# Three projections of a GEGLU feed-forward block: 2x2 blocks by seven products of block sums in place of eight block products

## The chip, the cores and the metric

The kernel runs on one core of one Trainium2 chip. The metric is the device time of one execution in microseconds (us); a run's state is told from its time and from the clock granted to TensorE. Below, "head" is what runs before the loop over column blocks or pairs, and "tail" what follows the last matmul. Engines are named PE (TensorE matmul), PEld (TensorE weight load, which overlaps PE), DVE (VectorE), ACT (ScalarE), POOL (GpSimd) and SP (SyncE, which here only issues DMAs). "Bank" is one of the eight PSUM banks of 128 x 512 fp32.

## The reference

```python
B, S, D, F = 32, 32, 1024, 3584            # all inputs bfloat16, normal * 0.05
def reference(x, w_gate, w_up, w_down):
    return (gelu_tanh(x @ w_gate) * (x @ w_up)) @ w_down
```

There are N = B*S = 1024 tokens. In units of 128x128 weights by 512 moving columns, gate and up cost 28 column blocks x 2 matrices x 2 token halves x 8 contraction blocks = 896 matmuls, and down costs 8 token blocks x 2 column halves x 28 contraction blocks = 448.

## The kernel before

The first four column blocks of gate and up run while inputs still arrive. Then comes one column block after the other, with the weights as the stationary operand, and both token halves after one weight load (`held` means that the weights stay in the array; this cut and the next have comments added):

```python
for m in range(4, FM):                      # FM = 28 column blocks of 128
    b0 = 4 * (m % 2)
    for kind, b in (("g", b0), ("u", b0 + 1)):
        for k in range(DK):                 # DK = 8
            for h in range(2):
                mm_gu(kind, m, h, k, b + 2 * h, held=h == 1)
    for h in range(2):
        glu(m, h, b0 + 2 * h, b0 + 2 * h + 1)   # ACT: gelu(bank) to SBUF; DVE: times bank -> hT
    # ... DMA loads of later weights (cut)

jobs = [[(tc, 0, 512), (tc, 512, 512)] for tc in range(TC - 1)]
jobs += [[(TC - 1, 0, 512)], [(TC - 1, 512, 416)], [(TC - 1, 928, 96)]]
for job in jobs:
    for m in range(FM):
        for i, (tc, col, n) in enumerate(job):
            # matmul: hT block (tc, m) stationary, wd[m] moving, held for the second column half
            ...
    # ACT or DVE copies each bank to SBUF as bfloat16, SP sends it out (cut)
```

## Time and profile before

| quantity | value | view |
|---|---|---|
| time | 299.25 us, median of 4 (299.12 to 299.92) | runs beside the changed kernel |
| span of the profiled execution | 297.9 us | page |
| PE busy, DVE busy, ACT busy | 294.5, 42.7, 37.3 us | page, engines |
| matmuls of the program | 1372, worth 1344 of 512 columns | page, groups |
| gate and up after the first 4 blocks | 33.1 to 198.9 us: 165.7 us | starts in the timeline |
| down, PE only | 198.9 to 295.6 us: about 96.7 us | starts in the timeline |

From the page of the kernel before: the engines (busy us, share of the span, instructions), the granted clock in 40 slices, and the chain that ended last ("issue" is time in which the profile shows nothing to wait for; a q after an engine means its sequencer).

```profile
PE 294.5 (99%) x1388; PEld 77.9 (26%) x808; DVE 42.7 (14%) x68; ACT 37.3 (13%) x67; POOL 0.7 (0%) x6
...
PEclk9999999999999999999999999999999999999999
...
PE 96%; DMA 2%; SPq 0%; issue 0%; ACT 0%
```

The list of waits of PE (engine, line, waited for: us in total, times, longest):

```profile
PE ps L98 <- PEq L310: 0.8, 1, 0.8
PE ps L98 <- DMA xT<-in_x_dram: 0.5, 1, 0.5
```

Groups of instructions with the shapes kept apart (count after the x; then busy us and mean ns of one; then idle time before them and what ended it):

```profile
L98 PE MATMUL ps<-xT,wg 128*128 128x512 bf16 x256 | 90.4, 380 | 0.5 <-DMA xT<-in_x_dram 0.5
...
L163 PE MATMUL ps<-xT,wg 128*128 128x512 bf16 x192 | 72.8, 379 | 0.0
...
L98 DVE TENSOR_TENSOR hT<-g,ps 128x512 bf16<-128x512 f32 x56 | 36.3, 685 | 159.0 <-PE ps L98 159.0
...
L98 PEld LDWEIGHTS ps<-xT,wg 128*128 128x128 bf16 x256 | 25.0, 98 | 72.4 <-issue 64.0 <-DMA wg<-in_w_gate_dram 1.0 <-DVE xT L98 0.3
...
L98 DVE CAST xT<-ps 128x512 bf16<-128x512 f32 x7 | 4.8, 692 | 79.8 <-ACT xT L98 79.8
...
L98 DVE CAST xT<-ps 128x416 bf16<-128x416 f32 x1 | 0.6, 592 | 9.8 <-PE ps L98 9.8
```

A matmul's record lasts 380 ns, but records overlap; what it costs is the distance between starts. The timeline of PE (start, length, what, count) shows that:

```profile
12.38 1.03 PE L98 MATMUL ps<-xT,wg 128*128 128x512 bf16 x4
13.24 1.03 PE L98 MATMUL ps<-xT,wu 128*128 128x512 bf16 x4
```

Four matmuls take 13.24 - 12.38 = 0.86 us; by the finer start times it is 0.2158 each, which the prediction takes as 0.2157. 1344 of them are 289.9 us. PE has nothing to wait for, so the span is a count of matmuls times 0.2157, plus about 8 us at the two ends. Held matmuls (line 163) and those with a weight load (line 98) last the same: the load of 98 ns is hidden.

### The profile page before, as it was taken

The numbers are of one execution on the slowest core, as the hardware profiler recorded it, in microseconds if no ns is written. First come the engines' busy times: TensorE is split into PE (matmuls) and PEld (weight loads), VectorE is DVE, ScalarE is ACT, GpSimd is POOL, SyncE is SP. The second block draws the span as 40 slices with busy tenths as digits, with TensorE's granted clock in tenths as the row PEclk, the third lists the DMA queues.
The fourth block names the chain that finished last, engine by engine and source line by source line (L and its number), as shares of the span: only waits on it lengthen the run. The fifth ranks groups of instructions, "written<-read, shape, count | busy, mean of one in ns | idle before, by whom it ended". The sixth has DMA issues, their size and how long they took to land.

```text
span 297.9 us, 2578 instructions
## 1 busy us (share of the span) xinstructions
PE 294.5 (99%) x1388; PEld 77.9 (26%) x808; DVE 42.7 (14%) x68; ACT 37.3 (13%) x67; POOL 0.7 (0%) x6
## 2 busy tenths in 40 slices
PE   8999999999999999999999999999999999999997
PEld 4444322222222222222222222222222222222244
DVE  1030311111222111111111122110000000000000
ACT  1030411111111111121111111110000000000010
POOL 0000000000000000000000000000000000000000
PEclk9999999999999999999999999999999999999999
DMA  7999743005707509312030030000101101011011
GB/s 164 275 216 357 246 153 108 35 0 187 236 2 264 160 1 315 109 50 91 0 132 11 0 141 0 0 2 0 35 0 35 37 0 35 0 37 35 0 35 35
DMA packets 28874, 26.37 MB, mean 89 GB/s; under 512 B 8384, under 2 KB 25280, under 8 KB 28864
## 3 DMA queue, kind: packets, MB, share of 16 engines
q1 hardware_dynamic: 26640, 24.25, 26.2%
q10 hardware_dynamic: 2224, 1.97, 2.7%
q8 instruction: 8, 0.13, 0.2%
q14 instruction: 2, 0.02, 0.0%
HBM read 22.28 MB, written 2.10 MB: 82 GB/s over the span
## 4 chain that ended last, share of the span: by engine, by line
PE 96%; DMA 2%; SPq 0%; issue 0%; ACT 0%
PE ps L98 54%; PE ps L163 42%; DMA xT<-in_x_dram 2%; SPq L98 0%; ACT xT L98 0%
## 5 line engine op out<-in xcount | busy, mean ns | idle before, releaser
L98 PE MATMUL ps<-xT,wg 128*128 128x512 bf16 x256 | 90.4, 380 | 0.5 <-DMA xT<-in_x_dram 0.5
L98 PE MATMUL ps<-xT,wu 128*128 128x512 bf16 x256 | 90.2, 379 | 0.0
L98 PE MATMUL ps<-wd,hT 128*128 128x512 bf16 (+2 forms) x280 | 86.6, 358 | 0.0
L163 PE MATMUL ps<-wd,hT 128*128 128x512 bf16 x196 | 74.3, 379 | 0.0
L163 PE MATMUL ps<-xT,wg 128*128 128x512 bf16 x192 | 72.8, 379 | 0.0
L163 PE MATMUL ps<-xT,wu 128*128 128x512 bf16 x192 | 72.8, 379 | 0.0
L98 DVE TENSOR_TENSOR hT<-g,ps 128x512 bf16<-128x512 f32 x56 | 36.3, 685 | 159.0 <-PE ps L98 159.0
L98 ACT ACTIVATE g<-ps 128x512 f32<-128x512 f32 x56 | 30.8, 595 | 159.3 <-PE ps L98 159.3
L98 PEld LDWEIGHTS ps<-wd,hT 128*128 128x128 bf16 x280 | 26.0, 98 | 71.4 <-issue 65.8
L98 PEld LDWEIGHTS ps<-xT,wg 128*128 128x128 bf16 x256 | 25.0, 98 | 72.4 <-issue 64.0
L98 PEld LDWEIGHTS ps<-xT,wu 128*128 128x128 bf16 x256 | 25.1, 98 | 71.6 <-issue 64.1
L98 DVE CAST xT<-ps 128x512 bf16<-128x512 f32 (+1 forms) x8 | 5.4, 679 | 89.6 <-ACT xT L98 79.8
L98 ACT ACTIVATE xT<-ps 128x512 bf16<-128x512 f32 (+1 forms) x9 | 5.0, 559 | 94.6 <-PE ps L98 94.6
L98 PE MATMUL ps<-const-bfloat16-1.0 128*128 128x512 bf16 (+1 forms) x8 | 2.9, 548 | 0.8 <-PEq L310 0.8
L98 ACT ACT_TABLE_LOAD x1 | 1.3, 1283 | 4.8 <-issue 4.8
L98 PEld LDWEIGHTS ps<-const-bfloat16-1.0 128*128 128x128 bf16 x8 | 1.0, 140 | 2.4 <-issue 2.4
L98 DVE COPY xT<-ps 128x256 bf16<-128x256 bf16 x4 | 0.9, 292 | 4.0 <-PE ps L98 4.0
L98 PE MATMUL ps<-ident,xn 128*128 128x128 bf16 x8 | 1.1, 314 | 0.0
L98 PEld LDWEIGHTS ps<-ident,xn 128*128 128x128 bf16 x8 | 0.9, 144 | 0.0
L98 POOL TENSOR_SCALAR_AFFINE_SELECT ident<-ident 128x128 bf16<-128x128 bf16 x1 | 0.3, 294 | 0.2 <-POOL ident L98 0.2
L98 POOL MEMSET ident<- 128x128 bf16 x1 | 0.2, 205 | 0.3 <-POOLq L310 0.3
L98 ACT ACTIVATE warm<-const-float32-0.0 128x1 f32<-128x1 f32 x1 | 0.2, 203 | 0.0
(4 smaller groups left out, 0.4 us busy)
## 6 DMA issues: line engine op xcount, KB each, us to landing
wd<-in_w_down_dram SPq DMA_DIRECT2D x7, 1024.0 KB, 5.4
wg<-in_w_gate_dram SPq DMA_DIRECT2D x6, 1024.0 KB, 7.8
wu<-in_w_up_dram SPq DMA_DIRECT2D x6, 1024.0 KB, 9.7
out_dram<-xT SPq DMA_DIRECT2D x15, 128.0 KB, 1.7
wu<-in_w_up_dram ACTq DMA_DIRECT2D x4, 128.0 KB, 5.0
wg<-in_w_gate_dram ACTq DMA_DIRECT2D x2, 256.0 KB, 5.5
wu<-in_w_up_dram ACTq DMA_DIRECT2D x2, 256.0 KB, 5.9
wg<-in_w_gate_dram SPq DMA_DIRECT2D x2, 128.0 KB, 3.4
```

The costliest lines, as they stand in the source:

```text
L98: ins = name(eng, *args, **kw) if callable(name) else getattr(eng, name)(*args, **kw)
L163: return eng.add_instruction(mybir.InstMatmult(start_tensor_calc=start, stop_tensor_calc=stop, ldweights=False, name=nc.get_next_instructi ...
```

## The change

The intent is to spend idle DVE and ACT time to remove PE work. A product of 2x2 blocks needs seven block products if sums of blocks are multiplied (Winograd's form of Strassen's method). With A for the activations and W for the weights:

```
S1 = A21+A22   S2 = S1-A11   S3 = A11-A21   S4 = A12-S2
T1 = W12-W11   T2 = W22-T1   T3 = W22-W12   T4 = W21-T2
P1 = A11 W11   P2 = A12 W21  P3 = S4 W22    P4 = A22 T4   P5 = S1 T1   P6 = S2 T2   P7 = S3 T3
C11 = P1+P2    U = P1+P6     V = U+P7
C12 = U+P5+P3  C22 = V+P5    C21 = V+P4
```

The first four column blocks stay as they were. The other 24 form 12 pairs (left, right); rows are the token halves. In down the rows are token halves, the columns the output halves, and the contraction is split in two sets of 14 blocks. Products 1 and 2 read raw bfloat16 blocks. Products 3 to 7 read sums kept in float32r, and where one operand is raw, ACT first copies it to float32r. P1, U and V are needed twice. ACT copies P1 and U from one bank to another, and matmuls add to both; V is read by DVE before P4 is added to its bank. (In down P7 is made early and DVE adds it to a copy of U.) Core of the diff, with lines joined or left out and comments added:

```diff
-        wg_b = [sb(f"wg{i}", [P, DK, GW * P], BF16) for i in range(NWB)]
+        S = sb("S", [P, 20, 512], F32R)         # sums of activations
+        T = sb("T", [P, 8, 2, 4, P], F32R)      # sums of weights, 8 units
...
+        def sums_w(p, u, at):                   # at: place in the engine's order, in us
+            if u == 0:   tt(o, blk(0, 1), blk(0, 0), SUB, at)
+            elif u == 1: tt(o, blk(1, 1), f(0), SUB, at)
+            elif u == 2: tt(o, blk(1, 1), blk(0, 1), SUB, at)
+            elif u == 3: act(o, blk(1, 1), COPY, at)
+            else:        tt(o, blk(1, 0), f(1), SUB, at)
...
+        A, E, B, C = (0, 1), (2, 3), (4, 5), (6, 7)   # banks for gate, up
+        for p in range(NP):                     # 12 pairs
+            def product(n, j, bank, start):     # j: gate or up
+                for k in range(4):
+                    if n == 1:   a, b = w[:, 0, j, k, col], x0[:, k, :]
+                    elif n == 2: a, b = w[:, 0, j, k + 4, col], x0[:, k + 4, :]
+                    else:
+                        s, u = {3: (3, 3), 4: (4, 4), 5: (0, 0), 6: (1, 1), 7: (2, 2)}[n]
+                        a, b = T[:, unit(p, u), j, k, :], S[:, 4 * s + k, :]
+                    mm(bank, a, b, start and k == 0, k == 3, add=not start)
+            product(1, 0, A[0], True)
+            act(bank(B[0]), bank(A[0]), COPY, at(1))
...
+            product(6, 0, B[0], False)
+            act(bank(C[0]), bank(B[0]), COPY, at(6))
...
+            product(7, 0, C[0], False)
+            tt(g22, bank(C[0]), p5[0], ADD, at(9.1))
+            act(g22, g22, GELU, at(10))
...
+            if p + 1 < NP:
+                for u in range(3):
+                    sums_w(p + 1, u, at(0.5 + 1.5 * u + (5.5 if p == 0 else 0)))
+                sums_w(p + 1, 3, at(8.5))
+                sums_w(p + 1, 4, at(7 if p else 9.05))
...
+        F, H = 0.2266, 0.216                    # us of a float32r and a bfloat16 matmul, for the order
+        sweep(1, PA, ...); sweep(2, PA, ...)    # down: 4 token blocks x 14 contraction blocks each
+        sweep(7, PA, ...); sweep(5, PA, ...); sweep(6, PB, ...); sweep(3, PB, ...); sweep(4, PA, ...)
```

Per pair PE has 56 matmuls (16 bfloat16, 40 float32r) in place of 64. No weights are held any more.

## The prediction

> **What bounds the kernel now.** TensorE. The page's engine table has PE busy 294.5 of 297.9 us, granted clock 1.000; the list of waits shows PE waiting 0.5 us for data and 0.8 us at start. In the timeline four 512-column matmuls take 0.86 us: 0.2157 each. There are 1372, worth 1344 full ones: 289.9 us. The other 8 us are head and tail. DVE (42.7 us) and ACT (37.3 us) are mostly idle, DMA averages 89 GB/s. Only less PE work helps, and DVE and ACT have room to pay for it.
>
> **What the change does.** The first 4 column blocks (128 matmuls) stay. The other 24 form 12 pairs of 56 matmuls in place of 64. Down becomes 7 products x 4 x 14 = 392 in place of 448. Total 1192, 152 fewer (11.3%). Products of raw blocks stay bfloat16 (432); products of sums are float32r (760). No trace of this case shows a float32r matmul. The kernel's own schedule counts 0.2266 us for one, 0.216 for bfloat16; I take that as its author's measurement. The Trainium skill, "TensorE: Matmul & The Clock Gate", section on weight-path perf modes, says fast weight load gives fp32 nothing and is off for it, so a dearer weight load is plausible; it still fits under a matmul. Every weight is loaded anew (no held matmuls), which cost nothing before (379 ns records either way).
>
> PE: 432 x 0.2157 + 760 x 0.2266 = 265.4 us, 24.5 less (33 less if float32r cost no more).
>
> **Added.** Per pair DVE makes 4 sums of 128x1024 into fp32. From CASTs of 416 and 512 columns (592, 692 ns) I estimate 1.22 us each; "VectorE: DVE Perf Modes", perf-mode tier table, also has fp32 tensor_tensor at 1x. Plus 8 operations of about 0.69: 10.4 us of a pair's 12.5. ACT: ten of 0.6 plus one of 1.0, 7 us. Both fit, with bank copies given at least a product's length (0.9 us) before their reader. In down DVE makes 56 sums (68 us) and about 14 bank operations (10 us) in 88 us, with buffers that make it wait for PE's first float32r sweep. By the order of instructions, the last sums of two sweeps come about 1 us before PE needs them: tight, so 0 to 3 us of stalls. Weights come in 512-byte rows, 2 MB per two pairs (25 us); before moved up to 357 GB/s: enough.
>
> **Sum.** Pairs start at 33.2 us (head as before); 12 x 12.5 = 150.2; down 112 x 0.2157 + 280 x 0.2266 = 87.6; PE ends near 271. Tail: copy 0.7, output DMA 1.7, signalling 0.3. Span 273.7, time 1.4 above the span as before, plus about 1.5 of stalls: **276.5 us**, range 273.5 to 284. Chances: faster 0.94, within 2% 0.03, slower 0.03.
>
> **What shows it right.** 1192 matmuls plus warm-up; float32r ones starting 0.226 us apart; pairs 12.5 us long with no PE waits above a few tenths; sums 1.22 us; DVE busy above 80% in the pair and down stages; PE waits, if any, on DVE at the start of the pairs and in sweeps 6 and 4 of down; granted clock still 1.0.
>
> **What would make it wrong.** Float32r at another rate (each 10 ns is 7.6 us; several passes would make it far slower); sums slower than 1.22 us, which makes DVE the limit of down; a throttled clock; bubbles at each switch of type or each wait (about 170 products); late weight rows.

## The result

277.6 us, median of 4 (276.78 to 277.84), against 299.25 us of the kernel before in the same rounds: a ratio of 0.9268, 95% interval 0.9251 to 0.9285. A ratio here is the mean time of one kernel's fast runs over the mean of the other's from the same rounds, so it is not quite the ratio of the medians quoted. The result was correct.

The page of the changed kernel, the same lines:

```profile
PE 270.6 (98%) x1191; PEld 184.4 (67%) x1208; DVE 208.2 (75%) x234; ACT 118.1 (43%) x180; POOL 0.7 (0%) x6
...
PEclk9999999999999999999999999999999999999999
...
PE 95%; DMA 2%; issue 1%; SPq 0%; DVE 0%
```

PE's waits:

```profile
PE ps L117 <- PEq L526: 0.8, 1, 0.8
PE ps L117 <- DMA arena<-in_w_gate_dram: 0.2, 1, 0.2
PE ps L117 <- DMA arena<-in_x_dram: 0.2, 1, 0.2
```

Groups, float32r being shown as f32 or fp32r:

```profile
L117 PE MATMUL ps<-S,T 128*128 128x512 f32 x480 | 118.4, 400 | 0.0
L117 PEld LDWEIGHTS ps<-S,T 128*128 128x128 f32 x480 | 90.0, 188 | 21.5 <-DVE tmp L117 0.8
...
L117 DVE TENSOR_TENSOR T<-arena 128x1024 fp32r<-128x1024 bf16 x38 | 45.8, 1217 | 7.4 <-PE ps L117 7.4
```

The chain of work in order of time (start, length, what, count), some of its pieces:

```profile
46.69 12.55 PE ps L117 x55
59.24 0.07 issue
59.31 12.54 PE ps L117 x55
71.85 0.07 issue
71.92 12.54 PE ps L117 x55
...
206.96 66.04 PE ps L117 x291
273.02 0.69 DVE arena L117
```

DVE went from 42.7 to 208.2 us and ACT from 37.3 to 118.1, yet the chain is still PE. A piece is one pair (its first matmul record is missing): 59.31 - 46.69 and 71.92 - 59.31 are 12.6 us each. Pairs run from 33.0 to 185.1 us, 152.1 us where the kernel before took 165.7: 13.6 us won. Down takes 87.7 us of PE where it took 96.7: 9 us won. About 0.8 us is given back in the tail (3.1 us in place of 2.3): the kernel before finished with a copy and a transfer of only 96 columns (0.25 and 1.4 us), this one with 512 (0.69 and 1.7 us).

One stage has a visible wait. This is the timeline of the first pair, with DVE's last sum for the second pair, then its bank operations, and the weight loads that wait for them:

```profile
42.36 1.22 DVE L117 TENSOR_TENSOR T<-arena,T 128x1024 fp32r<-128x1024 bf16 x1
43.49 1.88 DVE L117 TENSOR_TENSOR tmp<-ps,tmp 128x512 f32<-128x512 f32 x3
...
44.23 0.76 PEld L117 LDWEIGHTS ps<-S,T 128*128 128x128 f32 x4 [0.35 <-DVE tmp L117]
...
45.43 0.77 PEld L117 LDWEIGHTS ps<-S,T 128*128 128x128 f32 x4 [0.44 <-DVE tmp L117]
```

The first pair lasts 13.45 us by the starts of its weight loads, 0.85 more than the others. Some 0.2 us of that is no waiting: the pair's first load runs a whole matmul ahead of its matmul (33.01 and 33.22 us), that of the next pair hardly at all. By the starts of the matmuls about 0.65 us is lost.

### The profile page after: what moved, and what is told of

Same layout as the page of the kernel before. It is cut to its first block, busy times and chain, and to the rows that moved or that the text cites. A ratio compares the mean times of both kernels' runs of the same rounds, so it can differ in the third digit from the quotient of the medians.

```text
span 275.9 us, 3173 instructions
## 1 busy us (share of the span) xinstructions
PE 270.6 (98%) x1191; PEld 184.4 (67%) x1208; DVE 208.2 (75%) x234; ACT 118.1 (43%) x180; POOL 0.7 (0%) x6
## 4 chain that ended last, share of the span: by engine, by line
PE 95%; DMA 2%; issue 1%; SPq 0%; DVE 0%
PE ps L117 95%; DMA arena<-in_x_dram 2%; SPq L117 0%; DVE arena L117 0%
## 5 line engine op out<-in xcount | busy, mean ns | idle before, releaser
L117 PE MATMUL ps<-S,T 128*128 128x512 f32 x480 | 118.4, 400 | 0.0
L117 PEld LDWEIGHTS ps<-S,T 128*128 128x128 f32 x480 | 90.0, 188 | 21.5 <-DVE tmp L117 0.8
L117 PE MATMUL ps<-arena 128*128 128x512 bf16 x306 | 71.1, 379 | 1.4 <-DMA arena<-in_w_gate_dram 0.2
L117 ACT ACTIVATE tmp<-ps 128x512 f32<-128x512 f32 x64 | 38.3, 598 | 69.7 <-PE ps L117 69.5
L117 ACT ACTIVATE ps<-ps 128x512 f32<-128x512 f32 x56 | 32.4, 581 | 52.6 <-PE ps L117 50.2
L117 DVE TENSOR_TENSOR T<-arena,T 128x1024 fp32r<-128x1024 bf16 x38 | 46.2, 1222 | 11.5 <-PE ps L117 11.1
L117 DVE TENSOR_TENSOR T<-arena 128x1024 fp32r<-128x1024 bf16 x38 | 45.8, 1217 | 7.4 <-PE ps L117 7.4
L117 PE MATMUL ps<-T,S 128*128 128x512 f32 x224 | 51.3, 390 | 0.0
L117 PEld LDWEIGHTS ps<-T,S 128*128 128x128 f32 x224 | 42.0, 188 | 8.8
L117 DVE TENSOR_TENSOR tmp<-ps,tmp 128x512 f32<-128x512 f32 x48 | 32.9, 689 | 12.9 <-PE ps L117 12.9
L117 PEld LDWEIGHTS ps<-arena,hT 128*128 128x128 bf16 x112 | 10.9, 98 | 13.2 <-issue 0.3
L117 DVE TENSOR_TENSOR S<-hT 128x1024 fp32r<-128x1024 bf16 x14 | 16.5, 1217 | 0.0
L117 ACT ACTIVATE T<-arena 128x1024 fp32r<-128x1024 bf16 x12 | 12.6, 1053 | 0.0
```

The lines of the kernel that those rows point to most:

```text
L117: ins = name(eng, *args, **kw) if callable(name) else getattr(eng, name)(*args, **kw)
```

## The experiments

The theory (A): PE stays the limit, and its time is the sum of the distances between matmul starts, 0.2157 us for a bfloat16 one and 0.2266 for a float32r one; DVE and ACT have just enough room. Rivals: the rate of the products comes from something else than the type (B); the sums on DVE are what holds the kernel (D); the float32r cost is the weight load (W) or the streaming of 4-byte columns (S). All kernels were run on one chip per batch beside the kernel before.

### Sums in float16, and in bfloat16

```diff
-        S = sb("S", [P, 20, 512], F32R)
-        T = sb("T", [P, 8, 2, 4, P], F32R)
-        Sf = S[:, :, :].bitcast(FP32)            # and Tf, T2f likewise
+        S = sb("S", [P, 20, 512], F16)           # second kernel: BF16
+        T = sb("T", [P, 8, 2, 4, P], F16)
+        Sf = S
```

> All sums in float16 in place of float32r, nothing else changed. Theory A (PE is the limit and its time is the sum of the matmul starts, 0.2157 us for a 16-bit one and 0.2266 for a float32r one): 760 x 0.0109 = 8.3 us less, plus about 1.1 us of slightly longer steps after a switch of type and up to 0.9 us of the first pair's wait for DVE, so 267 to 269.5 us, every 512-column matmul 0.2157 us after the one before. Theory B (the rate comes from something else in the products, such as adding to banks that ACT has copied): no less than 276 us and starts of 0.2266 us remain. If DVE takes its 2x mode on all-16-bit operands, a sum falls from 1.22 us to about 0.69 us.

> As the float16 run, with bfloat16 sums: the same time within 0.3 us (both 16-bit). The error against the reference should be larger than with float16 and float32r sums, as a sum then keeps 8 bits of mantissa in place of 11; by how much is what the run is for.

Float16: 267.86 us (5 runs, 267.63 to 267.97), ratio 0.8938 (0.8920 to 0.8957). Bfloat16: 267.55 us (4 runs, 266.96 to 267.95), ratio 0.8927 (0.8904 to 0.8949). Both passed the comparison with the reference. The results don't state the size of the error where it passes, so the question of how much worse bfloat16 is remains unanswered. Groups of the float16 run, then pieces of its chain of work in order of time:

```profile
L118 PE MATMUL ps<-S,T 128*128 128x512 f16 x480 | 107.5, 379 | 0.0
...
L118 PEld LDWEIGHTS ps<-S,T 128*128 128x128 f16 x480 | 47.0, 98 | 56.6
...
L118 DVE TENSOR_TENSOR T<-arena 128x1024 f16<-128x1024 bf16 x38 | 25.5, 684 | 18.5 <-PE ps L118 18.5
```

```profile
69.60 12.03 PE ps L118 x55
81.64 0.05 issue
81.69 12.03 PE ps L118 x55
...
199.96 62.98 PE ps L118 x291
```

A pair is now 81.69 - 69.60 = 12.09 us, which is 56 x 0.2158. So neither the bank copies nor the change between two 16-bit types costs PE anything. The last piece holds the same 291 matmuls as the last piece of the changed kernel, 280 of them of sums: (66.04 - 62.98) / 280 = 10.9 ns per matmul is the price of float32r. B falls. The two spans differ by 10.0 us: 3.05 in down, 0.3 in the head, which varies from profile to profile, and about 6.7 in the pairs (12 x 40 x 0.0109 = 5.2 for the type; 12 x 0.086 = 1.0 for slower float32r steps after bfloat16 ones, described below; about 0.4 of waiting in the first pair, where the float16 run still loses 0.2). DVE's sum fell from 1.22 to 0.68 us. The Trainium skill's "VectorE: DVE Perf Modes", perf-mode tier table, gives tensor_tensor 2x with bfloat16 SBUF operands and 1x with fp32 ones; that fits both runs, as the sums of the bfloat16 one took 684 to 689 ns too. In the steady pairs this faster DVE is worth nothing: the pair's length is explained by PE alone.

### What sets the float32r rate: fewer columns, fewer weights

Three kernels, all wrong; in the pairs only:

```diff
                     if n == 1: ...
+                    if n > 2:
+                        b = b[:, 0:384]      # e2_n384; 0:256 in e7_n256
+                        a = a[:, 0:64]       # e2_m64 in place of the line above
                     mm(bank, a, b, start and k == 0, k == 3, add=not start)
```

With 64 weight columns the output has 64 partitions, so that kernel also narrows the bank slice in `mm` (not shown).

> Wrong result on purpose: in the pairs every float32r matmul streams 384 columns in place of 512, with the same 128x128 weights. Theory W (the 0.2266 us of a float32r matmul is set by its weight load, 0.188 us in the trace plus a fixed gap): starts stay 0.2266 us apart. Theory S (it is set by streaming 4-byte columns): about 3/4, 0.170 us, or as low as the weight load allows, 0.19 to 0.20 us. Pairs last 12.6 us by W, 11.3 us or a bit less by S.

> Wrong result on purpose: in the pairs every float32r matmul loads 64 weight columns in place of 128 and streams 512 columns. Theory W (weight load sets the pace): the load record falls to about half of 0.188 us and starts move to 0.2157 us apart as for bfloat16. Theory S (streaming sets it): starts stay 0.2266 us apart.

> Wrong result on purpose: as the 384-column run, with 256 columns. That run gave starts 0.1733 us apart and the changed kernel 0.2267, both 13.3 ns above the columns at 2.4 per ns; bfloat16 starts lie 2.5 ns above. Fixed cost alone: 106.7 + 13.3 = 120 ns between starts within a product. If the float32r weight load (0.188 us a record, which did not bind at 384 columns) binds below that: more than 120 ns, up to 0.19 us. The pairs as a whole should then wait for DVE, which needs about 10 us per pair.

These were single looks (state unknown): 254.6, 278.55 and 246.87 us, all with wrong results as intended. What counts are the starts, in stretches where the granted clock was 1.00. The timeline of PE inside one stretch of float32r products, one fence per kernel; first the changed kernel, then 384 columns, 256 columns, and 64 weight columns:

```profile
66.70 4.47 PE L117 MATMUL ps<-S,T 128*128 128x512 f32 x19
```

```profile
84.76 3.45 PE L117 MATMUL ps<-S,T 128*128 128x384 f32 x19
```

```profile
81.12 2.56 PE L117 MATMUL ps<-S,T 128*128 128x256 f32 x20
```

```profile
89.75 3.62 PE L117 MATMUL ps<-S,T 128*64 128x512 f32 x15
```

Less the last record's length (0.389, 0.334, 0.283 and 0.390 us) and divided by the number of steps, that is 226.7, 173.1, 119.8 and 230.7 ns between starts. With 128 weight columns, each 128 moving columns are worth 53.3 to 53.6 ns, 0.417 ns a column, and 13.1 to 13.4 ns remain in all three sizes. In down of the kernel before, 512, 416 and 96 bfloat16 columns start 215.8, 175.9 and 42.5 ns apart: the same slope, and 2.5 ns remain. The 2.5 ns are what the Trainium skill's "TensorE: Matmul & The Clock Gate", section on the 56 ns gap, states. So float32r costs 10.6 to 10.9 ns per matmul whatever its moving columns. W falls: half of the weight columns gave no gain, although the load record did shrink, from 188 to 134 ns, and 120 ns between starts is less than the 188 ns record of one load. The steps even became a little longer: they went on swinging between 224 and 236 ns, as the changed kernel's do only for the first ten or so after bfloat16 products. S falls too: it asks for 170.0 and 113.4 ns at 384 and 256 columns. The first of these is too close to 173.1 to tell it from a fixed cost; the second is not. Which part of the instruction carries the fixed cost no run here shows.

The load record of the changed kernel stands above; this is that of 64 weight columns:

```profile
L117 PEld LDWEIGHTS ps<-S,T 128*64 128x64 f32 x480 | 64.4, 134 | 46.7 <-DVE tmp L117 0.9
```

The 256-column run also shows the other limit. Its pairs last 9.85 us while its PE work would take 16 x 0.2157 + 40 x 0.12 = 8.25 us, and PE's waits name DVE:

```profile
PE ps L117 <- DVE tmp L117: 12.7, 20, 2.8
```

In these pairs DVE waits for no other engine. So its work of one pair, with the short gaps before operations that need its own last result, is about 9.85 us, not the 10.4 us of the prediction.

### More work for DVE

```diff
+                for i in range(1):               # 3 in the second kernel
+                    sums_w(p + 1, 2, at(3.6 + 0.1 * i + (5.5 if p == 0 else 0)))
                 sums_w(p + 1, 3, at(8.5))
```

> Float32r kernel, with one more 128x1024 sum per pair on DVE (the third sum made twice; right result). DVE's work per pair rises from 10.4 to 11.6 us, under the pair's 12.6 us of PE. Theory A (PE is the limit, DVE has 2.2 us of room per pair): no change, at most 1.3 us in the first pair, where DVE is already late. Theory D (DVE's sums are what holds the kernel at 277.6): 11 x 1.22 = 13.4 us longer, about 291.

> As the run before with three more sums: 10.4 + 3.7 = 14.0 us of DVE per pair, over PE's 12.6. Theory A: DVE becomes the limit, pairs last 14.0 us, 11 x 1.4 = 15.6 us longer, about 293 to 295, and PE's waits name DVE. Theory D: 11 x 3.66 = 40 us longer, about 318.

One more sum: 278.21 us (4 runs, 278.04 to 278.62), ratio 0.9296 (0.928 to 0.9313), 0.6 more than the changed kernel's 277.6 (each beside its own runs of before, 299.26 and 299.25). The pairs from the second on still take 12.6 us; the first takes 14.6, which is 1.2 more than before; in the spans of the two profiles a head 0.6 us shorter hides half of that. Three more: 291.15 us (4 runs, 290.74 to 291.66), ratio 0.9728 (0.9707 to 0.9748). There the steady pairs last 13.63 us, and DVE is named. Its chain of work in order of time shows DVE between the pieces of PE, and its list of PE's waits, in the second fence, names DVE's bank operations:

```profile
86.03 1.22 DVE T L117
87.90 1.19 PE ps L117 x4
89.10 9.97 PE ps L117 x43
99.66 1.22 DVE T L117
```

```profile
PE ps L117 <- DVE tmp L117: 7.2, 9, 3.7
```

D falls: DVE is not the limit of the kernel as it stands, but its room is between one and three sums a pair. I expected 14.0 us and not 13.63, because I took 10.4 us for the pair's own work by adding record lengths. Where sums that don't depend on each other follow, one starts every 1.136 us though its record is 1.22 us long: 6 distances in 8.03 - 1.22 us here, in down of the changed kernel.

```profile
186.02 8.03 DVE L117 TENSOR_TENSOR S<-hT 128x1024 fp32r<-128x1024 bf16 x7
```

The added sums write the tile of the sum before them again, and they start 1.257 us apart, 3 distances in 4.99 - 1.22 us:

```profile
94.15 4.99 DVE L117 TENSOR_TENSOR T<-arena 128x1024 fp32r<-128x1024 bf16 x4
```

With 9.85 us from the 256-column run, 9.85 + 3 x 1.257 = 13.62 us, which is the measured pair.

### The order in the first pair

```diff
-                sums_w(p + 1, 4, at(7 if p else 9.05))
+                sums_w(p + 1, 4, at(7 if p else 14.2))
```

> Only DVE's order in the first pair changes: the last sum for the second pair comes after the first pair's bank operations in place of before. If the first pair's 13.5 us (against 12.6 of the others) are PE waiting for DVE's late bank operations: 0.5 to 0.9 us less. If they are something else, no change.

276.77 us (5 runs, 276.53 to 277.03), ratio 0.9248 (0.9231 to 0.9264); the interval overlaps that of the changed kernel, so the times alone don't settle half a microsecond. The trace does for the mechanism: by its weight loads the first pair takes 12.96 us in place of 13.45 (12.75 by its matmuls, so some 0.15 us of waiting is left), and DVE's bank operations now follow the third sum directly:

```profile
40.67 1.22 DVE L117 TENSOR_TENSOR T<-arena 128x1024 fp32r<-128x1024 bf16 x1
41.80 1.88 DVE L117 TENSOR_TENSOR tmp<-ps,tmp 128x512 f32<-128x512 f32 x3
```

The spans of the two profiles differ by 1.1 us, of which 0.5 is this; the rest is the head, as the pairs began at 32.45 us in this profile and at 33.0 in the other. Other profiles began them anywhere from 32.1 to 33.0 us with the same head.

### Down by eight products again

```diff
-        sweep(1, PA, True, ...)      # and the six other sweeps with their sums
+        for q, (i, j) in enumerate(((0, 0), (0, 1), (1, 0), (1, 1))):
+            banks = PA if q % 2 == 0 else PB
+            for half in range(2):    # 4 token blocks x 14 contraction blocks of each half, bfloat16
+                ...
```

> The down projection back to its 8 block products (448 bfloat16 matmuls), the pairs as in the changed kernel. If the two parts simply add up: 448 x 0.2157 - (112 x 0.2157 + 280 x 0.2266) = 9.0 us longer than 277.6, so 286.6 within 0.7. A rival, that the down stage hides stalls or contention of DVE and so gains less: under 285.

286.01 us (4 runs, 285.77 to 286.36), ratio 0.9556 (0.9539 to 0.9573): 8.4 us longer than the changed kernel. From the first to the last weight load of down it takes 96.3 us and the changed kernel 87.2, a difference of 9.05 against 9.0 computed; the spans differ by 8.7 us, as the head was 0.3 us shorter in this profile. The two halves of the change add up.

## Why the prediction was right

- **PE is the limit before and after.** Right: PE's waits total 1.3 us before and 1.2 us after (weight loads wait some 5 us for ACT, DVE and DMA, mostly hidden), and adding one sum a pair leaves the steady pair's length alone. With faster sums on DVE (float16) the pair is as long as its 56 matmul starts.
- **1192 matmuls, 265.4 us.** Right: 1191 of the 1208 (with 16 at the start) are in the trace, some records missing, and the steps are 0.2157 and 0.2267 us. The 24.5 us were the right size. That the schedule's constant 0.2266 was a measured one was an assumption, and much hung on it (each 10 ns is 7.6 us); the trace bears the value out.
- **A dearer weight load is plausible as the reason of 0.2266.** Wrong as a reason. The float32r load is indeed longer (188 against 98 ns), which fits the section on weight-path perf modes that the prediction cited, but it is hidden. The cost is about 11 ns per matmul, whatever the moving columns, and halving the weight columns does not lower it.
- **Pairs of 12.5 us, beginning at 33.2.** Nearly: 12.6 us from 33.0 on. The 0.09 us per pair above 12.515 lie in the first ten or so float32r steps after bfloat16 products, where single steps are 0.224 to 0.239 us and not 0.2267. With float16 sums this is gone. What causes it no run tells. The prediction had named bubbles at a switch of type only among what would make it wrong.
- **0 to 3 us of stalls, 1.5 taken.** The size came out near, with 0.65 us in the first pair, but the other 1.1 us are those slower steps and no stalls; that the two together come close to 1.5 is luck. The place was half right: DVE is late in the first pair as said, but down has no stall at all: its last 262 float32r matmuls start 226.7 ns apart on average. There DVE finished earlier than I worked out, as its sums start 1.136 us apart and I counted 1.22, which is 4.7 us over 56 sums.
- **DVE busy above 80%.** 79.7% of the stretch from 60 to 160 us, and about 83% of down's float32r part. The estimate of 1.22 us for a sum was right (1217 ns) as a record, too long as a distance between starts.
- **Down 87.6, end of PE near 271.** 87.7 us, from 185.1 to 272.8, later by what the pairs took more.
- **Tail.** 3.1 us against the 2.7 predicted from the last matmul to the end of the span, and the time is 1.7 to 1.8 above the span and not 1.4. The 1.4 came from a median time and the span of another execution; the runs of the kernel before that have both show 1.8 too. These few tenths, with the first pair and the slower steps, are the 1.1 us between 276.5 and 277.6.

The version with 16-bit sums beats both kernels: 267.86 us with float16. Float16 keeps three more bits of a sum than bfloat16 at the same time; whether either is accurate enough for a use other than this comparison would have to be measured.

## What to carry to other kernels

When one engine has no waits at all, a change that trades its work for work of idle engines can be costed as count times start-to-start distance; here that gave the answer to 0.4%, and the check is whether each helper's load per period stays below that engine's period (9.85 of 12.6 us here). Count helpers by the distance between starts, not by record lengths, and look at the first period separately, where the work of set-up and of the loop meet. Ask whether intermediate sums need 32 bits: with 16-bit sums this kernel gained a further 9.7 us, nearly half of what the seven products had won.

## What the Trainium skill lacked or had wrong

- "TensorE: Matmul & The Clock Gate" has no rate for float32r. Measured: 226.7, 173.1 and 119.8 ns between starts at 512, 384 and 256 columns, that is the 16-bit rate plus 10.6 to 10.9 ns per matmul. With 64 weight columns and 512 moving ones the steps swing between 224 and 236 ns, 230 on average: no gain.
- The same page, section on weight-path perf modes, has no time for a float32r load, and the page's formula for a load (columns / 1.2) has no term for the type. Measured: 188 ns for 128 columns and 134 for 64, against 98 ns for bfloat16 and float16; such loads still fed matmuls that started 120 ns apart, so a load's record is not the pace at which loads can follow each other.
- The same page, section on the back-to-back issue gap, gives about 131 ns per matmul as the sustained rate at N=512 with weight loads and calls 216 ns an over-count. Every bfloat16 and float16 stretch of 512 columns that was measured here ran at 215.8 ns, with held weights and without, as the page's own section on the 56 ns gap has it.
- "VectorE: DVE Perf Modes", section on the drain, has the next operation start when the pipe is empty and says that one that is not held starts earlier, but it gives no time for an operation that needs the result, or writes the tile, of the one before it. Measured: a float32r sum of 1.22 us was followed after 1.25 to 1.26 us by such a one, and after 1.136 us by an independent one.
